# Unit 0's triangular inverse, a column solve on VectorE and a merge, replaced by five squarings on TensorE

## The chip, the cores and the metric

The kernel runs on one core of a Trainium2 chip. The metric is the device time of one execution in microseconds (us), the median of several runs. Three runs of the kernel before are given: 1079.76, 1079.80 and 1079.98 us. The engines are named PE (TensorE), DVE (VectorE), ACT (ScalarE), POOL (GpSimd) and SP (SyncE, which here only issues DMAs).

## The reference

Two stages. The first is a recurrence over 768 tokens for 4 batches and 8 heads with a 40 x 40 state each; the second is a mixture of 4 experts over the 3072 x 320 result.

```python
for t in range(S):
    y[:, :, t] = np.einsum('bhd,bhde->bhe', rt, state)
    Sa = np.einsum('bhde,bhe->bhd', state, at)
    state_decay = state * wt[:, :, None, :] - np.einsum('bhd,bhe->bhde', Sa, bt)
    state = state_decay + np.einsum('bhd,bhe->bhde', vt, kt)
...
for e in range(E):
    h = np.maximum(x @ w1[e], 0.0)
    out += p[:, e:e + 1] * (h @ w2[e])
```

All of it is in float32. In each chunk of 64 tokens the vectors Sa depend on one another through a strictly triangular 64 x 64 matrix F, so that a chunk needs (I - F)^-1, or something that acts as it, on a right-hand side. For the first chunk the state is zero, and that right-hand side is E V alone (E are the masked products of a and k, V the values).

## The kernel before

**Tiling.** A unit is one chunk of 64 tokens for two batches (tokens of both on the 128 partitions) and 8 heads: 16 matrices of 64 x 64. There are 24 units; units 0 and 1 are the first chunk. `within(q)` (line 462) makes what a unit needs inside its chunk: G, the running products of the decay w (transposes at line 286, scan at line 512), their reciprocals (529), N and K (556, 561), a scaled by G (565), their transposes on PE (535), and the products F ("pfe", 585) and E ("pe", 598). `substitute(q, eng)` (638) gathers the diagonal 32 x 32 blocks of F (643, 651, 663, 667) and solves them column by column in Z, two columns at a time, 16 rounds of a multiply (681) and a reduction (692); units 0 and 1 do it on DVE, the others on POOL. `merge(q)` (704) turns the solved blocks (709, 710), places them in QT (716) and makes the off-diagonal block with two sets of matmuls (pY, pQ). `step(q)` (742) multiplies the inverse with the right-hand side ("psat", "pst"), makes the outputs Y and the new state ("pxr", "pdy", lines 800 to 835), and brings Y into xT, the input of the mixture ("pxT", 841 to 846). `mixture_of_unit` (914) and `mixture_of_chunk` (982) are the experts' dense products ("ph", "po", "p"): they need xT and are most of PE's work.

**Products of quadrants.** `quadrants` (443) issues 32 matmuls of 64 x 64 on four quarters of the PE array, into two PSUM banks. All matmuls are issued through one helper, so their line is always 110 (transposes on PE: 113).

**Order.** Instructions of one engine that are kept in program order run in the order in which the main sequence (lines 1127 to 1214) calls the generators with `run(gen, n)`, n stages at a time; all PE instructions are, and most of DVE's in the first units (`pin`). For later DVE work a list (`VECTOR_ORDER`) states the order, and a few more pairs are stated at line 1341. What isn't kept in order is placed by the tile framework's scheduler. Before the first dense product the sequence also issues dummy matmuls (`keep_warm`, in lots of 16, 10, 20, 8 and 10), sets constants for the placing of Y on POOL (`set_pick`, 164), and loads weights on SP's queue in pieces; the third piece waits for the first Y of unit 0 (line 1343).

**PSUM and tiles.** There are five banks with the tag "big" and three with "mm". The tiles that the change uses take tags of tiles that are idle in the beginning ("hs", "a6", "F", "step", "xT", "osb").

## Time and profile before

| what | number | from |
|---|---|---|
| median of the runs | 1079.8 us | times |
| span of the profiled execution | 1077.3 us | page |
| lying around the span (median less span) | 2.5 us | worked out |
| PE busy | 1062.5 us, 99% of the span | page |
| DVE, ACT, POOL busy | 758.3, 353.2, 494.3 us | page |
| matmuls "ph" (first dense product) | from 43.82 us on | timeline |
| unit 0: first F product, first multiply of the solve, last reduction | 13.43, 19.35, 29.84 us | timeline |
| unit 0: first "psat", first Y, "pxT" | 34.19, 40.03, 40.87 us | timeline |

The page gives no device time of the profiled execution besides its span, so a change of the span is carried over to the median as it is. In a group's line the columns are: line, engine, operation, output and inputs with their shapes, the number of instructions, busy time in us, mean ns of one, and the idle time before them with what ended it. In the timeline they are start, duration, line, operation and shapes, the number of instructions merged into the row, and in brackets the idle time before them. In a table by stage each engine's busy time (and number of instructions) stands in a row for a stretch of time; PEclk is the TensorE clock granted, 1.00 being full speed.

### The profile page before, as it was taken

The page shows a single profiled execution, that of the slowest core. Times are in us where ns is not written, and L with a number is a line of the kernel's source. Part 1 is how long each engine was busy: PE and PEld are TensorE (multiplying, and loading weights), DVE is VectorE, ACT ScalarE, POOL GpSimd, SP SyncE. Part 2 cuts the span into 40 slices and gives each one's busy share as a digit, 9 for nine tenths or more (in the row PEclk, how much of TensorE's full clock was granted, in tenths as well). Part 3 has the DMA queues.
Part 4 walks back from the last instruction along what each step waited for, and adds up shares of the span by engine and source line. Part 5 has one row for each costly group of instructions (what it writes and reads, how often), then busy time and mean ns, then how long its engine had stood idle before and what let it go on. Part 6 is the DMA issues. An engine that isn't in the chain of part 4 may idle for free.

```text
span 1077.3 us, 38510 instructions
## 1 busy us (share of the span) xinstructions
PE 1062.5 (99%) x16140; PEld 955.1 (89%) x16140; DVE 758.3 (70%) x1549; ACT 353.2 (33%) x958; POOL 494.3 (46%) x1276
## 2 busy tenths in 40 slices
PE   7999999999999999999999999999999999999998
PEld 7878878899898999999999999999999999998887
DVE  7787679897676776876776768668767776634343
ACT  3433444422432423324333333233243333221110
POOL 5117777747254374363462653733735626520000
PEclk9999999999999999999999999999999999999999
DMA  7776644444444434443353263353343331121220
GB/s 129 192 202 129 142 108 108 101 85 102 103 103 104 104 92 85 115 99 79 91 129 80 59 155 62 83 128 81 90 106 86 96 89 58 54 82 42 84 76 13
DMA packets 258070, 105.81 MB, mean 98 GB/s; under 512 B 212536, under 2 KB 237672, under 8 KB 257896
## 3 DMA queue, kind: packets, MB, share of 16 engines
q1 hardware_dynamic: 253912, 102.51, 40.8%
q8 instruction: 127, 2.08, 0.8%
q10 hardware_dynamic: 3984, 0.84, 0.5%
q14 instruction: 47, 0.39, 0.1%
HBM read 95.40 MB, written 3.93 MB: 92 GB/s over the span
## 4 chain that ended last, share of the span: by engine, by line
PE 93%; DVE 3%; DMA 1%; ACT 1%; issue 1%; SPq 0%; POOL 0%; ACTq 0%; DVEq 0%
PE ph L110 40%; PE p L110 31%; PE pdy L110 3%; PE po L110 3%; PE pxr L110 2%; PE psat L110 2%; PE prn L110 2%; PE pfe L110 2%; PE pc L110 1%; PE pev L110 1%; PE pQ L110 1%; PE pe L110 1%; PE pNT L113 1%; PE pg L113 1%; PE pKT L113 1%; PE pY L110 1%
## 5 line engine op out<-in xcount | busy, mean ns | idle before, releaser
L698 POOL TENSOR_TENSOR Z<-Z 128x31 f32<-128x31 f32 (+7 forms) x704 | 263.8, 375 | 55.2
L1014 DVE TENSOR_TENSOR a<-hs 128x512 f32<-128x512 f32 x220 | 150.7, 703 | 111.6 <-ACT hs L888 111.6
L110 PE MATMUL ph<-xT,w1a 128*128 128x256 f32 (+3 forms) x1536 | 221.3, 374 | 1.7 <-issue 1.7
L888 ACT ACTIVATE hs<-ph 128x512 f32<-128x512 f32 (+1 forms) x208 | 116.9, 564 | 323.5 <-PE ph L110 323.1
L110 PE MATMUL ph<-xT,w1b 128*128 128x256 f32 (+3 forms) x1536 | 222.0, 374 | 0.0
L110 PEld LDWEIGHTS ph<-xT,w1a 128*128 128x128 f32 (+1 forms) x1536 | 167.9, 161 | 30.6 <-issue 9.5
L110 PEld LDWEIGHTS ph<-xT,w1b 128*128 128x128 f32 (+1 forms) x1536 | 168.8, 161 | 26.9 <-issue 6.1
L681 POOL TENSOR_TENSOR Z<-M,Z 128x62 f32<-128x62 f32 (+7 forms) x352 | 142.8, 406 | 98.0 <-DVE M L667 72.1
L110 PE MATMUL p<-sums,a 128*128 128x160 f32 x1056 | 164.9, 299 | 0.0
L903 DVE SCALAR_TENSOR_TENSOR osb<-p,gate,osb 128x320 f32<-128x320 f32 (+1 forms) x243 | 108.1, 481 | 79.2 <-PE p L110 72.9
L110 PEld LDWEIGHTS p<-sums,a 128*128 128x128 f32 x1056 | 152.8, 190 | 2.2
L648 POOL COPY below<-F 32x256 f32<-32x256 f32 x48 | 21.4, 445 | 227.5 <-ACT F L591 225.8
L110 PEld LDWEIGHTS p<-w,hs 128*128 128x128 f32 x704 | 98.6, 190 | 8.5 <-issue 7.3
L110 PE MATMUL p<-w,hs 128*128 128x160 f32 x704 | 104.9, 302 | 0.0
L110 PE MATMUL p<-w,a 128*128 128x160 f32 x704 | 102.8, 299 | 0.0
L110 PEld LDWEIGHTS p<-w,a 128*128 128x128 f32 x704 | 98.0, 190 | 0.0
L716 POOL COPY QT<-QTc 32x256 f32<-32x256 f32 x96 | 40.3, 420 | 71.6 <-DVE QTc L710 65.3
L808 ACT COPY RS<-pxr 64x256 f32<-64x256 f32 x88 | 32.3, 367 | 101.2 <-DVE SX L460 78.8
L629 ACT COPY EV<-pev 64x160 f32<-64x160 f32 x96 | 23.1, 286 | 90.5 <-PE pev L110 90.1
L529 DVE RECIPROCAL gp<-gp 128x320 f32<-128x320 f32 x24 | 51.6, 2152 | 0.7
L651 DVE STREAM_TRANSPOSE M<-blocks 128x1024 f32<-128x1024 f32 x24 | 47.3, 1969 | 2.9 <-ACT blocks L643 2.8
L460 DVE COPY_PREDICATED VC<-mask_up,pc 128x256 f32<-128x256 int32 x48 | 18.7, 443 | 38.4 <-PE pc L110 38.4
(153 smaller groups left out, 1389.4 us busy)
## 6 DMA issues: line engine op xcount, KB each, us to landing
w1a<-in_moe_w_dram SPq DMA_DIRECT2D x37, 512.0 KB
w1b<-in_moe_w_dram SPq DMA_DIRECT2D x37, 512.0 KB
w<-in_moe_w_dram SPq DMA_DIRECT2D x4, 1280.0 KB
w1a<-in_moe_w_dram SPq DMA_DIRECT2D x74, 64.0 KB
w1b<-in_moe_w_dram SPq DMA_DIRECT2D x74, 64.0 KB
natW<-in_w_dram SPq DMA_DIRECT2D x48, 80.0 KB
natB<-in_b_dram SPq DMA_DIRECT2D x48, 80.0 KB
natK<-in_k_dram SPq DMA_DIRECT2D x48, 80.0 KB
```

The costliest lines, as they stand in the source:

```text
L110: return stated(nc.tensor.matmul(**k))
L113: return stated(nc.tensor.transpose(**k))
L529: pin(noted(nc.vector.reciprocal(out=gp[:], in_=gp[:]), "1/gp", q.u))
L629: nc.scalar.copy(out=of_slot(q.EV[half(p)], i ^ p)[:, :, 0:D], in_=pev[i][half(p)])
L651: ins = nc.vector.transpose(out=M[:], in_=cols)
L681: ins = eng.tensor_tensor(out=Z[:, 1:3, 0:n, j + 1:Q], in0=M[:, j:j + 2, None, j + 1:Q].to_broadcast([P, 2, n, m]), in1=Z[:, here, 0:n, j: ...
L698: eng.tensor_tensor(out=z[:, 0], in0=z[:, 0], in1=z[:, x], op=ALU.add)
L716: ins = nc.gpsimd.tensor_copy(out=q.QT[quarter(i), :, quarter(i % 2)], in_=QTc[quarter(i)])
L808: nc.scalar.copy(out=RS[half(s), x ^ s::2], in_=prs[x][half(s)].rearrange("p (j i) t -> p j i t", i=2),)
L888: ins = nc.scalar.activation(out=h[:, i * HF // 2:(i + 1) * HF // 2, 0:n], in_=ph[i][:], func=ACTF.Relu,)
L903: ins = nc.vector.scalar_tensor_tensor(out=to, in0=p, scalar=sc, in1=to, op0=ALU.mult, op1=ALU.add)
L1014: ins = nc.vector.tensor_tensor(out=t[:], in0=x, in1=y, op=op)
```

## The change

For unit 0 alone the column solve, the merge and the separate products are gone. With F strictly lower triangular of size 64, (I - F)^-1 is the product of (I + F^(2^k)) for k = 0 to 5. `first_chain` makes F and its transpose U with masks on DVE, squares both five times with `quadrants` (the last time U alone), adds the unit matrix to each U on POOL (`plus_one`), and applies the factors to E V one after the other (`applied`). The factors 0 to 4 are applied there; the last one takes the place of QT in "psat" and "pst" of `step`. Copies out of PSUM are dealt to ACT (bank 0) and DVE (bank 1).

Besides that, unit 1's part of `within` is cut into more stages (its reciprocal in two halves, its transposes of V and R behind them), and the main sequence deals these stages between unit 0's. The dummy matmuls after the first two lots are gone, the constants of `set_pick` are made in two parts, and the loads of unit 2's raw w come later on SP's queue, behind the first two weight pieces. In `step`, unit 0's state update is a stage of its own behind Y. The state, unit 1's solve and everything from the first dense product on stay as they are.

```diff
+    lowf = sb.tile([P, L], FP32, name="lowf", tag="s", bufs=3)
+    nc.vector.memset(lowf[:], 1.0)
+    eye = sb.tile([P, L], FP32, name="eye", tag="xT", bufs=2)
+    nc.gpsimd.memset(eye[:], 0.0)
+    for q in range(2):
+        o = slice(q * L, (q + 1) * L)
+        nc.gpsimd.affine_select(
+            out=lowf[o], in_=lowf[o], pattern=[[-1, L]], compare_op=ALU.is_gt, fill=0.0, base=0, channel_multiplier=1,
+        )
+        nc.gpsimd.affine_select(
+            out=eye[o], in_=eye[o], pattern=[[-1, L]], compare_op=ALU.not_equal, fill=1.0, base=0, channel_multiplier=1,
+        )
...
     def set_pick():
         nc.gpsimd.memset(pick, 0.0)
...
+                    yield
...
+    tc.keep_in_program_order(nc.vector.tensor_copy(out=mask_low[:], in_=lowf[:]))
...
+    def half_at(k, s, i):
+        return i ^ (s & k & 1)
+    def at_level(t, k, j, s, i, n=64):
+        slot = half_at(k - 1, s, i) if k else s
+        return t[half(half_at(k, s, i)), slot, j, 0:n]
+    def first_chain(q, NT, KT, places, masks):
+        pairs = []
+        def pair():
+            t = sb.tile([P, HF, 2 * P], FP32, name="FU", tag="hs", bufs=3)
+            pairs.append(four_halves(t[:]))
+            return t
+        nc.gpsimd.memset(pair()[:], 0.0)
+        yield
+        def engines():
+            return enumerate((nc.scalar.copy, nc.vector.tensor_copy))
+        def out_of(to, p, n=L):
+            for r, move in engines():
+                tc.keep_in_program_order(move(out=to[:, r, :, 0:n], in_=p[r]))
+        def squared(name, k, lhs, rhs):
+            return quadrants(banks(name), 0, BY_TOKENS, L, lambda j, s, i: (
+                half_at(k, s, i), half_at(k + 1, s, i), j, at_level(lhs, k, j, s, i), at_level(rhs, k, j, s, i),
+            ))
+        def plus_one(k):
+            t = sb.tile([P, 2 * NJ, L], FP32, name="UI", tag=("a6", "F")[k % 2])
+            ins = nc.gpsimd.tensor_tensor(
+                out=t[:], in0=pairs[k][:, 1].rearrange("p r j e -> p (r j) e"),
+                in1=eye[:, None, :].to_broadcast([P, 2 * NJ, L]), op=ALU.add,
+            )
+            tc.keep_in_program_order(ins)
+            return in_slots(t[:])
+        def applied(k, x, to):
+            p = quadrants([of_mixture(f"px{r}") for r in range(2)], 0, BY_TOKENS, D, lambda j, s, i: (
+                half_at(k, s, i), half_at(k + 1, s, i), j, at_level(one_plus[k], k, j, s, i),
+                at_level(x, k, j, s, i, D),
+            ))
+            out_of(to, p, D)
+            return to
+        tc.keep_in_program_order(nc.scalar.copy(out=q.VC[:, :, 0:D], in_=n_tokens(q)))
+        pf = quadrants(banks("pfe"), 0, BY_TOKENS, L, lambda j, s, i: (
+            s, i, j, of_slots(q.AT, s, j, i), of_pairs(NT, s, j, i),
+        ))
+        pu = quadrants(banks("pu"), 0, BY_TOKENS, L, lambda j, s, i: (
+            s, i, j, of_pairs(NT, s, j, i), of_slots(q.AT, s, j, i),
+        ))
+        pe = quadrants([of_mixture(f"pe{r}") for r in range(2)], 0, BY_TOKENS, L, lambda j, s, i: (
+            s, i, j, of_pairs(KT, s, j, i), of_slots(q.AT, s, j, i),
+        ))
+        for to, data, mask in ((pairs[0][:, 0], pf, mask_low), (pairs[0][:, 1], pu, mask_up)):
+            for r in range(2):
+                ins = nc.vector.copy_predicated(
+                    out=to[:, r], mask=mask[:, None, :].to_broadcast([P, NJ, L]), data=data[r],
+                )
+                tc.keep_in_program_order(ins)
+        one_plus = [plus_one(0)]
+        ET = ETs()
+        for s in range(2):
+            tc.keep_in_program_order(causal(of_slot(ET[:], s), pe[s]))
+        VT = sb.tile([P, 2 * NJ, L], FP32, name="VT", tag="turned", bufs=3)
+        q.RT = sb.tile([P, 2 * NJ, L], FP32, name="RT", tag="RT", bufs=2)
+        moves = []
+        for x, t, p in (("V", VT, big("pVT")), ("R", q.RT, of_mixture("pRT"))):
+            turn(f"p{x}T", tok(q.n["padded" + x]), False, p)
+            for at, (o, p_) in enumerate(places(t, p)):
+                moves.append(lambda o=o, p_=p_, x=x, at=at: tc.keep_in_program_order(
+                    noted(nc.scalar.copy(out=o, in_=p_), x + "Tc", q.u, at)))
+        for move in moves[:3]:
+            move()
+        yield
+        X = None
+        for k in range(4):
+            F, U = pairs[k][:, 0], pairs[k][:, 1]
+            p = squared("pfe", k, U, F), squared("pu", k, F, U)
+            pair()
+            for x in range(2):
+                out_of(pairs[k + 1][:, x], p[x])
+            one_plus.append(plus_one(k + 1))
+            if k < 3:
+                moves[3 + k]()
+            if k == 0:
+                q.EV = EVs()
+                pev = [of_mixture(f"pev{r}") for r in range(2)]
+                for j, s, i in BY_TOKENS:
+                    at = (s * NJ + j) * D
+                    matmul(
+                        out=pev[i][half(i), at:at + D], lhsT=ET[half(i), head(j, s), :],
+                        rhs=q.VC[half(i), head(j, s), 0:D], start=True, stop=True,
+                    )
+                X = in_slots(q.EV[:])
+                for i, move in engines():
+                    ins = move(
+                        out=X[half(i), :, :, 0:D],
+                        in_=pev[i][half(i), 0:H * D].rearrange("p (r j e) -> p r j e", r=2, j=NJ),
+                    )
+                    tc.keep_in_program_order(ins)
+            else:
+                to = sb.tile([P, 2, NJ, 64], FP32, name="X", tag="step", bufs=3)
+                X = applied(k - 1, X, to[:])
+            yield
+        F, U = pairs[4][:, 0], pairs[4][:, 1]
+        pu = squared("pu", 4, F, U)
+        pair()
+        out_of(pairs[5][:, 1], pu)
+        q.one_plus = plus_one(5)
+        to = sb.tile([P, 2, NJ, 64], FP32, name="X", tag="step", bufs=3)
+        X = applied(3, X, to[:])
+        yield
+        pc = quadrants(banks("pc"), 0, BY_TOKENS, L, lambda j, s, i: (
+            d_half(j, s), i, j, of_slots(VT, d_half(j, s), j, i, D), of_slots(q.RT, d_half(j, s), j, i, D),
+        ))
+        q.X = applied(4, X, in_slots(RHs()[:]))
+        yield
+        masks(pc)
+        yield
...
         if q.u == 1:
-            yield
-            VT = turn_rv("V")
-            yield
-            turn_rv("R")
             yield
...
         pg = turn("pg", tok(Gv), q.u == 2, of_mixture("pg") if q.u == 1 else None)
+        if q.u == 1:
+            yield
         pg = by(pg[:], 64)[:, :, 0:D]
         gp = sb.tile([P, H, D], FP32, name="gp")
         pin(noted(nc.vector.tensor_tensor(out=gp[:], in0=pg, in1=n["W"][:], op=ALU.mult), "gp", q.u))
-        pin(noted(nc.vector.reciprocal(out=gp[:], in_=gp[:]), "1/gp", q.u))
-
-        yield
+        for hs in (slice(0, NJ), slice(NJ, H)) if q.u == 1 else (slice(0, H),):
+            pin(noted(nc.vector.reciprocal(out=gp[:, hs], in_=gp[:, hs]), "1/gp", q.u))
+            yield
+        if q.u == 1:
+            VT = turn_rv("V")
+            yield
+            turn_rv("R")
+            yield
...
+        if q.u == 0:
+            yield from first_chain(q, NT, KT, places_of, masks)
+            return
...
-            RH = q.EV
+            RH = q.EV if q.u else None
...
+        def rhs_at(j, s, i, n=64):
+            return RH[half(i ^ s), head(j, s), 0:n] if q.u else at_level(q.X, 5, j, s, i, n)
+        def inverse_at(j, s, i):
+            return q.QT[half(i ^ s), head(j, s), :] if q.u else at_level(q.one_plus, 5, j, s, i)
         psa = quadrants(p, 0, BY_TOKENS, L, lambda j, s, i: (
-            i ^ s, d_half(j, s), j, RH[half(i ^ s), head(j, s), :], q.QT[half(i ^ s), head(j, s), :],
+            i ^ s, d_half(j, s), j, rhs_at(j, s, i), inverse_at(j, s, i),
         ))
         SX = SXs()
         if not q.end:
-            at = (banks("pst"), 0) if q.start else (p, NJ * L)
+            at = (p, NJ * L)
+            if q.start:
+                at = (banks("pst") if q.u else [of_mixture(f"pst{x}") for x in range(2)], 0)
             pst = quadrants(*at, BY_TOKENS, D, lambda j, s, i: (
-                i ^ s, i, j, q.QT[half(i ^ s), head(j, s), :], RH[half(i ^ s), head(j, s), 0:D],
+                i ^ s, i, j, inverse_at(j, s, i), rhs_at(j, s, i, D),
             ))
...
             noted(nc.vector.tensor_tensor(out=Y[:], in0=Y[:], in1=Gv, op=ALU.mult), "YG", q.u)
+        if q.u == 0:
+            yield
         if not q.end:
...
     norm = normalize()
+    pick_set = set_pick()
     keep_warm(16)
     run(ws[0], 1)
     go(load_raw(units[1], "W"))
     run(ws[0], 1)
     keep_warm(10)
     run(ws[0], 1)
-    run(ws[1], 1)
     for x in "VR":
         load_padded(units[1], x)
     load(units[1], "WBK")
     go(load_raw(units[1], "A"))
-    go(load_raw(units[2], "W"))
     load_probs()
     load_piece()
     load_piece()
     load_w2(order_of(-1)[0])
+    run(ws[0], 1)
+    run(pick_set, 9)
+    run(ws[0], 1)
+    def scores_of(u):
+        run(ws[u], 1)
+        yield
+    run(ws[0], 1)
+    run(ws[1], 1)
+    go(load_raw(units[2], "W"))
     load_piece()
     load_piece()
     run(ws[0], 2)
-    keep_warm(20)
-
-    def scores_of(u):
-        run(ws[u], 1)
-        yield
-
-    substitute(units[0], nc.vector, scores_of(0))
+    run(ws[1], 1)
     run(ws[0], 1)
-    set_pick()
-    m, s = merge(units[0]), begin_step(0)
-    run(m, 1)
+    run(ws[1], 1)
     run(ws[0], 1)
-    keep_warm(8)
-    run(norm, 1)
-    run(ws[1], 1)
-    keep_warm(10)
     load(units[2], "W")
     for x in "VR":
         load_padded(units[2], x)
-    run(m, 1)
+    run(ws[1], 1)
+    run(ws[0], 1)
+    run(pick_set)
+    run(ws[1], 1)
+    run(ws[0])
+    s = begin_step(0)
+    run(s, 2)
+    go(load_raw(units[2], "A"))
+    run(norm, 1)
+    run(s, 1)
     run(ws[1], 2)
-    run(ws[0])
-    run(ws[1], 2)
-    run(m)
-    go(load_raw(units[2], "A"))
-    run(s, 3)
     run(ws[1], 1)
     run(s, 1)
     run(ws[1], 1)
+    run(s, 1)
     run(s)
+    run(ws[1], 1)
     load(units[2], "BK")
     load_w2(order_of(-1)[1])
     load_piece()
...
-    for one, then in [*zip(names, names[1:]), *((f"out{n}", x) for n, x in moved), ("blocks0.3", "VCv1"), ("blocks0.3", "ETc0.0"), ("blocks1.3", "Zu1.0"), ("blocks1.3", "Zu1.3"), *turned_ahead, *in_second, *waits_of_scalar]:
+    for one, then in [*zip(names, names[1:]), *((f"out{n}", x) for n, x in moved), ("SXc0.3", "VCv1"), ("SXc0.3", "VTc1.0"), ("blocks1.3", "Zu1.0"), ("blocks1.3", "Zu1.3"), *turned_ahead, *in_second, *waits_of_scalar]:
```

## The prediction

> **What bounds the kernel now.** The page first: PE is the bound, but a busy PE is not the whole answer, because dummy matmuls count as busy.

> ```profile
> PE 1062.5 (99%) x16140; PEld 955.1 (89%) x16140; DVE 758.3 (70%) x1549; ACT 353.2 (33%) x958; POOL 494.3 (46%) x1276
> ```

> So I cut the span where the first dense product "ph" starts, 43.82 us, in the table by stage (columns: stretch, then PE, PEld, DVE, ACT, POOL busy, clock, DMA).

> ```profile
> 0.00:43.82 43.82, 36.68 (x600) 33.48 (x604) 34.50 (x84) 17.45 (x48) 20.50 (x60) 0.96 0.75 153
> 43.82:200.00 156.18, 154.78 (x2670) 129.49 (x2660) 122.09 (x249) 61.48 (x180) 91.98 (x229) 1.00 0.59 139
> 600.00:800.00 200.00, 200.00 (x3172) 182.71 (x3171) 149.28 (x304) 68.80 (x188) 95.26 (x249) 1.00 0.43 99
> ```

> Behind 43.82 us PE is idle for 1.4 us in the next 156 and not at all later; its order is fixed and its work there isn't changed. So the time is "when the first ph starts, plus a constant", and the question is when it starts. The chain of waits (start, duration, what) tells what leads up to it:

> ```profile
> 13.43 0.77 PE pfe L110 x32
> ...
> 17.90 0.70 DVE Z L663
> ...
> 29.92 0.11 DVE Z L692
> ...
> 30.71 0.45 DVE QTc L710
> ...
> 32.96 0.41 POOL QT L716
> ...
> 37.15 0.46 DVE SX L460
> ...
> 44.00 5.30 PE ph L110 x64
> ```

> The reader is to see that from 14 to 31 us the chain is DVE's solve of unit 0, then the merge, then the step. Every microsecond taken out of this stretch lets ph start earlier, as long as unit 1's pc and pfe, which stand ahead of ph in PE's order (42.38 to 43.8), come earlier too.

> **What goes.** From F's arrival in PSUM (14.17) to the mask SX (37.15) the chain takes 22.98 us: blocks, M and its products to 19.3; 16 rounds to 30.03; Qc, QTc and the merge to 34.2; psat and pxr to 37.15. The first three go. ACT's copies and POOL's select of ET go as well (1.3 us on POOL, off the path), and 38 of the dummy matmuls, which filled idle time.

> **What comes, step by step**, with these rows (mean ns behind the bar):

> ```profile
> L501 DVE COPY RT<-pRT 128x256 f32<-128x256 f32 x1 | 0.4, 424 | 3.3 <-PE pRT L113 3.3
> L460 DVE COPY_PREDICATED VC<-mask_up,pc 128x256 f32<-128x256 int32 x10 | 3.9, 441 | 4.1 <-PE pc L110 4.1
> L565 POOL TENSOR_TENSOR AT<-AT,G 128x512 f32<-128x512 f32 x1 | 1.3, 1280 | 0.0
> ```

> A set of 32 quarter matmuls follows the next after 0.46 us (pfe 42.89, pe 43.36), and its result is in PSUM 0.74 us after its start (13.43 to 14.17).
> 1. Masked copies of F and U: four on DVE, two take 0.78: 1.6 us. First squaring at 15.8. ACT's VT copies, PE's transposes of V and R and DVE's ET lie beside.
> 2. One level: F's product, U's product behind it (ready after 1.20), DVE's copy of U 0.42, 0.05 to PE: 1.7 us. Level 0 has the pev matmuls behind it on two quarters only; not shown before, between 0.46 (four quarters) and 0.92. I take 0.9: level 0 is 1.8 us, to 17.6.
> 3. Level 1: DVE runs EV's copy (0.45), then unit 1's moved G transposes (0.93), gl and G0 (0.27), from 17.8 to 19.45, before it copies F and U (0.84): to 20.3. The move costs 1.0 us; before, these sat in a gap at 13.29.
> 4. Level 2: to 22.0.
> 5. Level 3: DVE copies X (0.3), then unit 1's scan (1.24; before, it sat behind QTc). The scan reads two SBUF operands, and POOL's addition "I + U" of this level starts at the same moment. What happens then is in the timeline:

> ```profile
> 37.29 1.28 POOL L565 TENSOR_TENSOR AT<-AT,G 128x512 f32<-128x512 f32 x1
> 37.83 1.09 DVE L556 SCALAR_TENSOR_TENSOR n_tok<-natB,gp 128x320 f32<-128x320 f32 x1
> ```

> The same n_tok took 0.49 us at 11.49, with only the 0.37 us selects on POOL; here it ends 0.35 after POOL's. So the scan is taken to wait for POOL, 0.95 us (bounds: nothing, and 1.28): scan to 24.5, copies to 25.35. POOL's addition with a broadcast operand isn't in the trace; I take 1.28, the row of the same shape, between the memset of that shape (0.53) and 1.4 (512/320 of k_tok's 0.87).
> 6. Level 4, U alone: X (0.3), unit 1's AT transpose (0.70), U's copy 0.42 to 26.8, the last addition 1.28 to 28.05. Beside it pg, pc and the last `applied` on PE.
> 7. psat from 28.1: 0.74, SaT 0.65, pxr 0.74: 30.35. DVE meanwhile: gp 0.45, half the reciprocal 1.08, VC's masks 0.78: 30.4. SX mask at 30.4, against 37.15: 6.75 us earlier.
> 8. SX to Y (2.88) and to pxT (0.84) as before: pxT at 34.1. The second half of the reciprocal (1.08) lies in the 2.3 us of pdy; the transposes of unit 1's V and R lie between pxr and pdy, where PE waits for SX. Unit 1's N follows Y on DVE, K and its scaling of a run on POOL from 31.5 to 33.7.
> 9. Behind pxT (1.5): pNT, pKT (0.46 each), pc; NT's copy (0.59) comes behind xT's (0.48) on ACT, to 36.95; pfe, KT's copy, pe: ph at 38.1. Before, pNT and pKT came ahead of pxT, so pxT to ph took 2.95 us and now 4.0: 1.05 us are given back.

> Sum: 43.82 - 38.1 = **5.7 us earlier**. Span 1077.3 - 5.7 = 1071.6. The median of the runs lies 2.5 us above the span, and I carry that over: 1079.8 - 5.7 = 1074.1.

> **Edits costed at nothing.** PE's 480 added quarter matmuls lie in time in which PE waits or ran dummies; without that cover each 32 cost 0.46. POOL's new constants (a memset and four selects of 0.24) and the memset of FU (twice 0.53) end near 11.6, ahead of F; the nine pick steps behind (0.74 + 8 x 0.37) end near 15.3, ahead of the first addition at 15.8; if the scheduler puts the memset behind them, 1.1 us are lost. The other selects need to be done by pxT only. SP: unit 2's four raw w loads (0.49 each) go behind the probabilities and two pieces, which are issued some 2 us sooner; unit 1's raw a is issued by 19.9 as before and needed at 25.65. The stage between Y and the state update lets N pass in front of it; the state is first read by unit 2.

> **The clock.** One stretch speaks against the change:

> ```profile
> 9.52:12.93 3.41, 2.20 (x21) 2.02 (x19) 3.38 (x4) 1.62 (x5) 3.05 (x8) 1.00 1.03 122
> ...
> 19.75:23.16 3.41, 1.49 (x26) 1.07 (x17) 3.07 (x11) 3.13 (x10) 0.00 (x0) 1.00 0.70 126
> 23.16:26.57 3.41, 3.32 (x35) 3.20 (x36) 3.10 (x10) 0.04 (x1) 0.00 (x0) 0.50 0.55 154
> ...
> 36.80:40.21 3.41, 2.77 (x78) 2.26 (x72) 1.94 (x4) 1.80 (x6) 1.77 (x2) 1.00 0.48 81
> ```

> After 3.41 us with PE busy for 44%, the next 3.41 us ran at half clock; after 64% and 81% they did not. In my schedule levels 3 and 4 are the thin place: PE is busy 22.0 to 23.55 and from 25.35 on, so a stretch of 3.41 us has between 46% and 80%, by where it begins. A drop costs what PE has on the path in the next 3.41 us, about 1.5 us (two to three of psat, pxr, `applied`, at 0.46 to 0.74 each). [...]

> **Rivals.**
> - *One or two half-clock stretches* (1.5 us each): 1075.6 to 1077.1. For it: 46% beside 44%. Against: only some positions of the stretch give that, and the other levels are 65 to 90%.
> - *The waits at levels 1 and 3 don't come* (scan ahead of POOL's addition, pev at 0.46, the scheduler uses gaps): 1 to 2 us better: 1072.1 to 1073.1. Against: DVE's order is pinned.
> - *The gain is hidden by the weights*: ph starts early and waits for w1 or w2; at worst 1079.8. Against: the DMA share falls from 1.11 (35 to 36 us) to 0.40, so the first two pieces and w2 have landed by 36; issued 2 us sooner they have by 34, ahead of 38.1. The third piece waits for unit 0's Y, which moves 6.75 us, more than ph.
> - *The change does not do what it says*: DVE stays the chain's engine, since each level needs its copies. If all of unit 1's moved DVE work (4.8 us) came on the path instead of the 3.3 counted, 1075.6; in my range.
> - *Slower*: the half clock stays. PE's work on the path from 15.8 us on is 5 x 1.2 for the squarings, 2.2 (applied, psat, pxr), 2.3 (pdy), 1.5 (pxT), 2.3 (pNT to pe): 14.3 us, which would double: 1074.1 + 14.3 = 1088.4. It decides from 40% of that work on, four stretches in a row. Against: at half clock PE is busier, and the row above is back at 1.00 after one stretch.

> **Chances.** Forecast (1073.2 to 1075): 0.52. Half-clock stretches or all of DVE's moved work on the path: 0.26. Better than 1073.2: 0.10. Gain hidden: 0.06. Slower: 0.06. What a measurement here can tell from no change is about 0.2% (2.2 us), so up to 1077.6 counts as faster: 0.52 + 0.26 + 0.10 = 0.88, less 0.01 for a third stretch: 0.87; within 0.2%: 0.07; slower: 0.06. The range takes in both ends of the unknown costs: down to 1071.8 (scan's wait gone, pev at 0.46, the additions at half their price: together 2.3 us), up to 1077.3 (two stretches).

> **What would show it.** First squaring near 15.8 and the sixth product near 25.4; levels 1 and 3 longer than 0 and 2, with DVE's G and scan as what they wait for; the scan longer than 1.24 us beside a POOL addition; SX at 30.4, pxT at 34.1, ph at 38.1; PE still not idle behind it. Wrong would be: a clock below 1.00 between 26 and 34 us, levels of more than 3 us throughout, ph waiting for a DMA, or new idle time of PE behind ph.

## The result, and the profile after

The changed kernel takes 1089.45 us (median of four runs, 1086.8 to 1090.68), the kernel before 1079.89 us on the same chip: a ratio of 1.0072, 95% interval 1.0051 to 1.0093. It is slower by 0.7%, where 1074.1 us (1071.8 to 1077.3) was predicted. Its profiled execution took 1088.4 us with a span of 1086.7, against a span of 1077.3 before.

The page of the changed kernel, its line of engines and its line of the queue that brings instructions (packets, MB, share of 16 engines):

```profile
PE 1064.7 (98%) x16512; PEld 957.2 (88%) x16512; DVE 752.3 (69%) x1532; ACT 352.0 (32%) x953; POOL 497.9 (46%) x1280
...
q8 instruction: 130, 2.13, 0.8%
```

Of the first line nothing can be read: PE still seems busy all the time. The second is the one that the prediction passed over. 2.13 MB in 130 packets are 16 KB each. The same line before the change:

```profile
q8 instruction: 127, 2.08, 0.8%
```

The table by stage, cut at the same places as before:

```profile
0.00:43.82 43.82, 31.47 (x825) 29.00 (x827) 25.31 (x58) 14.08 (x38) 23.35 (x63) 0.84 0.63 131
43.82:200.00 156.18, 152.21 (x2756) 127.31 (x2748) 118.30 (x246) 62.45 (x183) 89.90 (x224) 1.00 0.60 141
600.00:800.00 200.00, 200.00 (x3169) 182.49 (x3168) 146.00 (x299) 67.23 (x183) 101.51 (x266) 1.00 0.41 94
```

In the first 43.82 us PE, DVE and ACT do less than before: PE 31.47 us in place of 36.68, DVE 25.31 in place of 34.50. The work did leave DVE, and yet ph starts later. The clock fell from 0.96 to 0.84. The chain of waits says what is there instead:

```profile
16.02 0.62 PE pfe L110 x32
16.64 0.34 PE pu L110 x21
16.98 0.92 issue
17.90 0.37 PE pu L110 x9
...
20.43 2.02 issue
22.45 0.42 PE px L110 x10
...
25.96 2.24 DVE G L666
...
30.02 1.80 issue
31.82 0.43 PE px L110 x11
...
35.20 1.14 PE psat L110 x32
...
36.71 1.90 issue
38.61 0.86 PE pst L110 x19
...
45.69 1.61 PE pxT L110 x12
...
49.72 5.41 PE ph L110 x64
```

"issue" is time in which the engine waits for nothing that the profile shows. In the sets' names pfe and pu are the products for F and U, px those of `applied`, pev is E V. Four times PE stops in the middle of a set of 32 matmuls whose operands are all there: 0.92 + 2.02 + 1.80 + 1.90 = 6.64 us. The places are regular. From 17.90 to 22.45 PE executes the last 11 of pu, 32 pev, 32 pfe, 32 pu and 20 of the 32 px: 127 matmuls, and with each its weight load, 254 instructions. Two more in the trace are semaphore instructions, which aren't counted as busy: 256. The stretches from there to 26.19, 31.82 and 38.61 have 127 matmuls and 256 instructions each as well, and one packet of q8 comes in each. It looks as if PE had used up a block of code and waited for the next; run 1 below puts that to the test. ph starts at 49.72 in place of 44.00 (both from the chain), 5.7 us later, where 5.7 us earlier was predicted.

The clock, in slices of one microsecond:

```profile
21.00:22.00 1.00, 0.00 (x0) 0.00 (x0) 0.79 (x3) 0.00 (x0) 0.00 (x0) 1.00 0.39 77
...
23.00:24.00 1.00, 1.00 (x48) 1.00 (x46) 0.36 (x2) 0.30 (x2) 0.76 (x1) 0.50 0.18 46
...
37.00:38.00 1.00, 0.00 (x0) 0.00 (x0) 0.26 (x1) 0.07 (x1) 0.00 (x0) 0.50 0.08 9
```

Half clock holds from about 22.6 to 26.0 and from 32.9 to 43.1 us. Ahead of the first stretch stands the stop of 2.02 us (slice 21); ahead of the second a wait of 1.29 us for DVE's copies (to 29.11) and the stop of 1.80. The stop at 36.71 (slice 37) lies inside the second.

Of the 9.4 us that the span grew, 5.7 are there when ph starts. The rest comes behind it, by the waits of both traces: near 90 us ph waits 1.0 us for a weight piece, near 121 us pxr 0.7 with no releaser, in the middle of a set; at 320 to 360 us PE's clock is 0.96 (1.00 before), which by half of its 3.4 us at half clock is an estimated 1.7.

### The profile page after: what moved, and what is told of

Same layout as the page of the kernel before. It is cut to its first block, busy times and chain, and to the rows that moved or that the text cites. A ratio compares the mean times of both kernels' runs of the same rounds, so it can differ in the third digit from the quotient of the medians.

```text
span 1086.7 us, 39253 instructions
## 1 busy us (share of the span) xinstructions
PE 1064.7 (98%) x16512; PEld 957.2 (88%) x16512; DVE 752.3 (69%) x1532; ACT 352.0 (32%) x953; POOL 497.9 (46%) x1280
## 3 DMA queue, kind: packets, MB, share of 16 engines
q8 instruction: 130, 2.13, 0.8%
## 4 chain that ended last, share of the span: by engine, by line
PE 95%; issue 1%; DVE 1%; ACT 1%; DMA 1%; SPq 0%; ACTq 0%; DVEq 0%
PE ph L110 40%; PE p L110 31%; PE pdy L110 3%; PE po L110 3%; PE pxr L110 2%; PE psat L110 2%; PE prn L110 2%; PE pfe L110 2%; PE pc L110 1%; PE pev L110 1%; PE pQ L110 1%; PE pe L110 1%; PE pg L113 1%; PE pNT L113 1%; PE pKT L113 1%
## 5 line engine op out<-in xcount | busy, mean ns | idle before, releaser
L110 PE MATMUL ph<-xT,w1a 128*128 128x256 f32 (+3 forms) x1536 | 222.2, 375 | 1.8 <-issue 1.8
L110 PE MATMUL ph<-xT,w1b 128*128 128x256 f32 (+3 forms) x1536 | 222.2, 374 | 0.0
L110 PEld LDWEIGHTS ph<-xT,w1a 128*128 128x128 f32 (+1 forms) x1536 | 168.6, 162 | 30.5 <-issue 10.7
L110 PEld LDWEIGHTS ph<-xT,w1b 128*128 128x128 f32 (+1 forms) x1536 | 169.1, 162 | 26.9 <-issue 5.9
L110 PE MATMUL p<-sums,a 128*128 128x160 f32 x1056 | 165.0, 300 | 0.0
L110 PEld LDWEIGHTS p<-sums,a 128*128 128x128 f32 x1056 | 152.8, 190 | 2.2
L110 PEld LDWEIGHTS p<-w,hs 128*128 128x128 f32 x704 | 98.6, 190 | 8.5 <-issue 7.3
L110 PE MATMUL p<-w,hs 128*128 128x160 f32 x704 | 104.9, 302 | 0.0
L110 PE MATMUL p<-w,a 128*128 128x160 f32 x704 | 102.8, 299 | 0.0
L110 PEld LDWEIGHTS p<-w,a 128*128 128x128 f32 x704 | 98.0, 190 | 0.0
L860 POOL COPY QT<-QTc 32x256 f32<-32x256 f32 x92 | 37.9, 412 | 58.7 <-DVE QTc L854 55.1
L686 DVE RECIPROCAL gp<-gp 128x320 f32<-128x320 f32 (+1 forms) x25 | 51.8, 2071 | 0.7
L476 DVE COPY_PREDICATED VC<-mask_up,pc 128x256 f32<-128x256 int32 x48 | 18.6, 442 | 40.1 <-PE pc L110 38.1
```

Of the source, the lines that this page charges most:

```text
L110: return stated(nc.tensor.matmul(**k))
L686: pin(noted(nc.vector.reciprocal(out=gp[:, hs], in_=gp[:, hs]), "1/gp", q.u))
L860: ins = nc.gpsimd.tensor_copy(out=q.QT[quarter(i), :, quarter(i % 2)], in_=QTc[quarter(i)])
```

## The experiments

TensorE's code is counted in instructions of the trace. An fp32 product of a quarter leaves four there, two matmuls and the weight load of each, so a set of 32 is 16 products and 64 instructions. "ph at" is the start of the first ph in the timeline (before 43.82, after 49.54). It and the stops are read from one profiled execution of each kernel; in runs 2, 5, 12 and 14 that was the longest of the kernel's executions (1092.36, 1094.43, 1090.04 and 1090.30 us), so there it stands for more than the median. A ratio is to the kernel before on the same chip, whose median lay between 1080.3 and 1081.8 us. A piece is half of one expert's w1, and w2 is an expert's second matrix.

**1. The added matmuls without their data.** The kernel before, with independent quarter matmuls of a constant in place of its 20 dummies, 8 sets of 32, and the same again late:

```
-    keep_warm(20)
+    quads(banks("quad"), 8)
...
+        if u == 8:
+            quads(banks("quad"), 8)
```

> The kernel before, with the 20 dummy matmuls of 128x128 at 14.5 us replaced by 8 sets of 32 independent quarter matmuls (256 matmul records with as many loads of weights, 3.7 us at 0.46 us a set), and 8 more such sets put among the dense products at about a third of the span. None of them waits for data, and none is read. Theory of the code blocks (in the profile of the changed kernel PE stops four times in the middle of a set, 128 records and 128 loads apart, 0.9 to 2.0 us each, and one 16 KB packet of the instruction queue lies ahead of each stop): both places show one or two stops of about 1 to 3 us with no releaser ('issue'), 128 records apart. Rival (the stops are waits for copies, or the draining of the array between shapes): the sets run without a stop, 3.7 to 4 us each lot. If the stops come only beside heavy DMA, the early lot has them and the late one, where the DMA share is about 0.4, doesn't.

Measured: 1092.69 us, one run. The timeline, early and late:

```profile
17.97 2.10 PE L110 MATMUL quad<-ident 64*64 64x64 f32 x128 [1.47 <-issue]
...
22.25 0.74 PE L110 MATMUL quad<-ident 64*64 64x64 f32 x34 [2.18 <-issue]
...
347.97 2.10 PE L110 MATMUL quad<-ident 64*64 64x64 f32 x128 [0.55 <-issue]
...
351.70 1.04 PE L110 MATMUL quad<-ident 64*64 64x64 f32 x56 [1.63 <-issue]
```

The matmuls wait for nothing and nothing waits for them, and PE still stops after each 128. 128 matmuls and their 128 weight loads are 256 instructions, and the packets of the instruction queue are 16 KB each. They last 2.10 us, and the next block starts 4.28 us (early, with a DMA share of 0.61 in between) or 3.73 us (late, with 0.26) after the one before. So a stop here is no wait for data: these quarter matmuls use up code faster than it comes. ph is at 46.54, 2.7 us later than before; where the rest of the 12.4 us of this one run comes from isn't followed here.

**2. Is it the clock?** Four dummies of 128x128, written into the bank that is used next, ahead of the squarings 2 to 5, psat, pxr and pxT:

```
-            return quadrants(banks(name), 0, BY_TOKENS, L, lambda j, s, i: (
+            p = banks(name)
+            held(p[0], hold)
+            return quadrants(p, 0, BY_TOKENS, L, lambda j, s, i: (
```

> The changed kernel, with 4 dummy matmuls of 128x128 (0.12 us each at full clock, 16 machine instructions) ahead of each squaring from the second on, of psat, pxr and pxT, written to the bank that the following set overwrites. Theory of the clock (PE below 46% busy in some stretch of 3.4 us halves the clock, and that is most of the loss): clock 1.00 through the chain, ph some 5 us earlier than 49.5, time near 1084. Theory of the code blocks (stops first, clock second): the stops stay, 1 to 2 us each, the clock may still drop, ph at 47 to 49, time 1086 to 1089.

Measured: 1089.35 us, ratio 1.0084 (1.0058 to 1.011); ph at 52.01. Both theories had ph earlier than that. The first stretch at half clock is gone, the second is not (34.7 to 44.9 us). It follows a longer stop than any in the changed kernel; the 28 dummies are 112 instructions of code themselves:

```profile
33.23 0.40 PE L110 MATMUL pu<-FU 64*64 64x64 f32 x12 [2.93 <-issue]
```

The clock as a cause by itself is not shown, and not excluded by this run.

**3. SP's order.** In the changed kernel SP stands 13.1 us, to 45.66, behind the third piece, which waits for unit 0's Y, and unit 2's loads stand behind it. Here they go ahead of the piece, as before the change:

```
+    load(units[2], "W")
+    for x in "VR":
+        load_padded(units[2], x)
     load_piece()
     load_piece()
```

> The changed kernel, with unit 2's loads of W, V and R put in the program ahead of the third weight piece. In the changed kernel SP's queue stood still from 32.9 to 45.66 us behind that piece, which waits for unit 0's Y, and these loads came behind it; later, at 90.4 us, ph waited 1.0 us for a piece. Theory that this order costs time behind the first ph: that wait goes, time 1 to 2 us lower; ph's start the same, or up to 1 us later, since the loads then lie beside the fetch of code. Rival (the late wait comes from ph's late start alone): no difference.

Measured: 1089.97 us, ratio 1.0098 (1.0077 to 1.0118), ph at 50.24. The 1.0 us wait at 90 us is gone, others came (ph for ACT's blocks 1.6, pdy for code 0.9), and the time is as before this edit. SP's order alone is not it.

**4. The weights later.** First piece behind the third squaring's copies:

```
-    for k, then in ((2, "Y0.0"), (served[22], "SX5.0")):
+    for k, then in ((0, "third0"), (2, "Y0.0"), (served[22], "SX5.0")):
```

> The changed kernel, with the first weight piece, and so everything behind it on SP's queue, waiting for the copies of the third squaring (about 25 us instead of 23.2). If the fetch of a code block is slowed by the weights' transfers on the same DMA engines (a block took 3.7 to 4.6 us from its predecessor's first instruction while the DMA share was 0.4 to 0.8, and 5.6 and 6.8 us while it was 0.9 to 1.1), the blocks up to the third squaring come as before or sooner and the later ones are slowed as much; ph changes by less than 1 us either way, and the stop in the middle of the last squaring's px shortens only if the weights start after its block was asked for. If the fetch doesn't depend on the transfers: the same four stops at the same places.

Measured: 1087.34 us, ratio 1.0064 (1.0049 to 1.0079); ph at 47.95, 1.6 us earlier, where less than 1 us was expected, with the first piece issued at 24.32 in place of 23.18. The stops are 1.04, 1.76, 1.48, 1.73 and 1.44, but the block that came at 31.82 comes at 30.50, and the first stretch at half clock is gone. Part of it is given back, po waits 1.9 us for w2.

**5. More code.** One more set of 32 quarter matmuls ahead of the squarings 2 to 5, 256 instructions:

```
+            if extra:
+                quads(p)
```

> The changed kernel, with one set of 32 independent quarter matmuls (64 machine instructions, 0.46 us of PE) ahead of each of the squarings 2 to 5, written to the banks that the squaring overwrites. The run with 4 dummies of 128x128 there (16 machine instructions, 0.47 us) had ph at 52.0 us in its profile. Theory of the code blocks: 256 machine instructions more are one block more, one stop more, and ph 4 us or more behind the changed kernel's 49.5, near 54; time near 1094. Theory that PE's or DVE's time sets the chain: PE's 0.46 us lies in the waits for the copies, as the dummies' did; ph and time within 2 us of the changed kernel.

Measured: 1091.09 us, ratio 1.0089 (1.0061 to 1.0116). One block more, a fifth stop (0.65, 1.70, 1.96, 2.51, 3.54), and ph at 54.38, 4.8 us later, as expected. The profiled execution took 1094.43 us, near the 1094 expected, but the median rose by less (1091.1).

**6. Less code.** The powers from the second on in bf16, whose product is one matmul and one load (sets of 16 in the trace), 224 instructions fewer in all:

```
-            t = sb.tile([P, HF, 2 * P], FP32, name="FU", tag="hs", bufs=3)
+            t = sb.tile([P, HF, 2 * P], BF16 if pairs else FP32, name="FU", tag="hs", bufs=3)
```

> The changed kernel, with the powers of F from the second on kept in bfloat16 for the squarings (the powers that are added to I and applied are rounded to bfloat16 too, which changes the result slightly). The trace shows an fp32 matmul of the program as two records and two loads; in bfloat16 it is expected as one of each, so the seven sets of the squarings 2 to 5 are 224 machine instructions less, 0.9 of a block. Theory of the code blocks: ph 3 to 4 us earlier, 45 to 46 us, time 1083 to 1086. Theory of the clock: PE does less, so the clock drops as before or more; ph 1 us earlier at most.

Measured: 1085.51 us, ratio 1.0035 (1.0021 to 1.0048), ph at 45.97, as expected. Stops 0.70, 0.29 and 1.32, but 17 us at half clock (23.0 to 40.1).

**7. Three squarings.**

```
-        for k in range(4):
+        for k in range(2):
...
-        F, U = pairs[4][:, 0], pairs[4][:, 1]
+        F, U = pairs[2][:, 0], pairs[2][:, 1]
```

> The changed kernel with three squarings instead of five: the factors of the 16th and 32nd power of F are left out of the product. That takes away six sets (squarings and applied), 384 machine instructions, 1.5 blocks, and by the prediction's own levels 3.35 + 2.7 us less what is left of unit 1's DVE work (2 us), 4 us. Theory of the code blocks: 1.5 blocks of 4.3 us, ph 6 us earlier, near 43.5, time near 1082. Prediction's theory alone: 4 us earlier, near 45.5.

Measured: 1083.85 us, ratio 1.0023 (1.0006 to 1.004), ph at 43.28, as expected. Stops of 0.77, 2.02, 1.09 and 1.18; 10.2 us at half clock (28.6 to 38.9). Even with two of five squarings gone, ph starts only where it did before the change.

**8. Both.** Three squarings and bf16 powers:

> Both: three squarings (the 16th and 32nd power's factors are left out) and bfloat16 powers from the second on (rounded). Three sets are 96 machine instructions less than with three squarings in fp32. Theory of the code blocks: another 1.5 us, ph near 42, ahead of the kernel before (43.8); time 1078 to 1081. Theory of the clock: no earlier than with three squarings.

Measured: 1082.01 us, ratio 1.0003 (0.9991 to 1.0015), no difference from before; ph at 43.08 where 42 was expected, and a time above the 1078 to 1081 expected. So 480 instructions fewer bring ph 6.5 us forward, but 13.7 us still lie at half clock (24.8 to 35.1, 38.5 to 41.9).

**9 and 10. The clock again, with less code.** Dummies in the places where run 6 and run 8 waited; for run 10, ahead of the third squaring, psat and pxT:

```
-        pu = squared("pu", 2, F, U)
+        pu = squared("pu", 2, F, U, 10)
...
+            held(p[0], 5)
...
+                held(px, 6)
```

> The changed kernel with the bf16 powers of the run with less code, and 128x128 dummies in the places where that run's TensorE waited: 10 ahead of the third squaring, 10 ahead of the fifth, 4 ahead of psat, 6 ahead of pxT. 30 dummies are some 120 machine instructions, under half a block. Without them: TensorE at half clock from 23.0 to 40.0 us, ph at 45.97, 1085.51 us. Theory 'blocks first, then the clock': with fewer instructions the half clock now has a price of its own, since TensorE's work between 23 and 40 us is one chain; the dummies keep the clock above 0.9 over 20 to 40 us, ph starts at 42 to 43.5, and the time is 1081 to 1083. Rival 'the stops alone': the clock is kept but ph stays within 1 us of 45.97 and the time within 1 us of 1085.5. Rival 'dummies do not keep the clock': the clock is half for over 8 us between 23 and 40 as without them.

> The run with three squarings and bf16 powers (it leaves out the factors with the 16th and the 32nd power), with dummies: 10 ahead of the third squaring, 5 ahead of psat, 6 ahead of pxT, some 84 machine instructions. Without them: half clock from 25 to 35.2 and 38.8 to 41.5 us, ph at 43.08, 1082.01 us, the same as the kernel before. Theory 'blocks first, then the clock': the clock stays above 0.9 over 20 to 40 us, ph starts at 38.5 to 40.5, and the time is 1078 to 1080, at or below the kernel before. Rival 'the stops alone': ph within 1 us of 43.1 though the clock is kept. Rival 'given back behind ph': ph earlier by 2.5 us or more, but the time within 1 us of 1082, with waits for weights behind ph in its place.

Measured: run 9 1086.81 us, ratio 1.0054 (1.0042 to 1.0066), ph at 45.88 (45.97 without the dummies); run 10 1082.33 us, ratio 1.0023 (1.0005 to 1.0042), ph at 43.44 (43.08). In run 9 the clock is 1.00 in every slice from 14 us to past ph. Its timeline has, at pdy:

```profile
38.86 0.46 PE L111 MATMUL pdy<-VC,k_tok 64*64 64x104 f32 x5 [3.10 <-issue]
```

and run 10's chain:

```profile
25.91 1.00 PE psat L111 x9
26.91 1.13 issue
28.04 0.69 PE psat L111 x32
...
31.42 0.59 PE pdy L111 x17
32.00 3.31 issue
35.32 1.69 PE pdy L111 x44
```

psat is back at 0.69 us (1.14 at half clock in the changed kernel). PE does these matmuls in little over half the time and then stands longer: 3.10 us at most in run 9, 1.32 in run 6. For run 9 "the stops alone" holds by ph and the clock; its time is 1.3 us off, on another chip. In run 10 ph fits that rival too, but the clock was kept only up to the stop of 3.31 us; then it dropped, here in a slice behind it:

```profile
36.00:38.00 2.00, 2.00 (x34) 1.75 (x26) 1.00 (x3) 0.00 (x0) 0.00 (x0) 0.57 0.03 8
```

The dummies are 120 and 84 instructions of code themselves, so these two runs can't say what the full clock would be worth if it cost no code.

**11 and 12. The blocks without the weights.** Runs 10 and 9, with the first piece behind ACT's copies of SaT:

```
-            nc.scalar.copy(out=SaT[:, :, x, :], in_=psa[x])
+            noted(nc.scalar.copy(out=SaT[:, :, x, :], in_=psa[x]), "SaTc", q.u, x)
...
-    for k, then in ((2, "Y0.0"), (served[22], "SX5.0")):
+    for k, then in ((0, "SaTc0.1"), (2, "Y0.0"), (served[22], "SX5.0")):
```

> The run with three squarings, bf16 powers and dummies (it leaves out the factors with the 16th and the 32nd power), with one more edit: the first weight piece is issued behind ACT's copies of SaT (about 29 us) in place of 22.5 us. Without it: the block of code that TensorE needs at pdy came while the DMA engines were busy for 97% and more with the weights (28 to 33 us), TensorE stood 3.31 us, ph at 43.44, 1082.33 us. Theory 'the blocks pace TensorE, and weights in flight slow the blocks': the stop at psat (1.13) and that at pdy (3.31) fall to under 0.5 and under 1.0 us, ph starts at 40 to 41.5, and the time is 1079 to 1081.5, the same as the kernel before, with up to 1 us of new waits for w2 or the third piece. Rival 'a block takes as long without the weights': the stop at pdy stays over 2.5 us and ph within 0.7 us of 43.4. Rival 'given back': ph at 41.5 or earlier, and a time within 1 us of 1082.3, with over 2 us of new waits for weights behind ph.

> The run with bf16 powers and dummies and all five squarings, with the same edit: the first weight piece behind ACT's copies of SaT (about 33 us). Without it: stops of 0.77, 0.33, 0.20 and 3.10 us, clock 1.00 throughout, ph at 45.88, 1086.81 us. Theory 'the blocks pace TensorE, and weights in flight slow the blocks': the stop at pdy falls to under 1.5 us, since only the last block is then requested beside the weights, ph starts at 43 to 44.5, and the time is 1084 to 1086. Rival 'a block takes as long without the weights': a stop of over 2.5 us stays and ph stays within 0.7 us of 45.9. Rival 'given back': ph at 44.5 or earlier, time within 1 us of 1086.8 or above, with over 2 us of new waits for weights behind ph.

Run 11's first ph and its second po, in the timeline:

```profile
37.20 2.60 PE L111 MATMUL ph<-xT,w1a 64*64 64x128 f32 x32
...
59.27 7.11 PE L111 MATMUL po<-w,hs 128*128 128x320 f32 x16 [6.14 <-DMA w<-in_moe_w_dram]
```

The stops at psat and pdy are gone altogether, and ph starts at 37.20, 6.2 us earlier than in run 10 and 6.6 earlier than before the change. The table by stage shows what was taken away (last columns: clock, DMA share, GB/s). Run 10, then run 11:

```profile
28.00:30.00 2.00, 1.96 (x88) 1.88 (x91) 0.19 (x1) 1.19 (x5) 0.00 (x0) 1.00 0.97 245
30.00:32.00 2.00, 2.00 (x53) 1.65 (x45) 1.52 (x3) 1.94 (x7) 0.00 (x0) 1.00 1.00 341
32.00:34.00 2.00, 0.00 (x1) 0.00 (x0) 0.29 (x1) 1.30 (x4) 1.63 (x2) 1.00 1.14 300
```

```profile
26.00:28.00 2.00, 1.97 (x73) 1.76 (x71) 1.97 (x4) 0.31 (x3) 0.00 (x0) 1.00 0.01 2
28.00:30.00 2.00, 2.00 (x51) 1.87 (x44) 0.81 (x3) 1.93 (x9) 0.00 (x0) 1.00 0.18 33
30.00:32.00 2.00, 2.00 (x68) 1.70 (x66) 1.21 (x2) 1.92 (x7) 0.71 (x1) 1.00 0.84 291
```

With the DMA engines nearly free while PE works up to psat (shares of 0.01 and 0.18 from 26 to 30 us, in run 10 0.75 and 0.97), PE stops nowhere there. And yet the run takes 1085.06 us, ratio 1.0035 (1.0021 to 1.005). From the first ph to the end its profiled execution takes 1046.3 us, the kernel before 1033.5. Of these 12.8 us po's wait for w2 is 6.1. In the wait and behind it the clock is half, from 57.6 to 64.5 us, and po takes 7.11 us (4.58 in the kernel before, at full clock):

```profile
60.00:64.00 4.00, 4.00 (x9) 2.63 (x8) 0.00 (x0) 0.00 (x0) 0.00 (x0) 0.50 1.07 313
```

Run 12, with five squarings, has no stop between 26 us and ph, and ph at 42.27 in place of 45.88; its profiled execution waits 2.2 us for w2 and 4.4 for a piece. It takes 1085.51 us, ratio 1.0045 (1.0028 to 1.0063). So the theory was right on the stops in both. Run 11's time misses its range and even what "given back" allowed (by 1.8 us); run 12's lies inside the theory's range, but with ph earlier than the theory had it and with the waits that "given back" names.

**13 and 14. Is that only the order of the loads?** Runs 11 and 12, with the second expert's w2 ahead of unit 2's loads:

```
+    load_w2(order_of(-1)[1])
     load(units[2], "W")
...
-    load_w2(order_of(-1)[1])
```

> The run with three squarings whose first piece is issued behind SaT (it leaves out the factors with the 16th and the 32nd power), with one more edit: the second expert's w2 is loaded ahead of unit 2's W, V and R (about 39 us) in place of behind all of unit 2's loads (52.09 us). Without it: ph at 37.20, but the second po waited 6.14 us for that w2, and 1085.06 us. Theory 'two walls, code blocks in front of ph and the weights behind it, and the second is only an order on the queue': the wait of 6.1 us is gone, ph stays at 37 to 38, and the time is 1078 to 1080.5, as the kernel before or up to 2 us below it. Rival 'the bytes bind': the second po still waits for over 2 us, or a wait for the third or fourth piece of over 2 us comes in its place, and the time stays at 1082 or above.

> The run with all five squarings, bf16 powers, dummies and the first piece behind SaT, with the same edit: the second expert's w2 ahead of unit 2's W, V and R (about 43 us) in place of 53.79 us. Without it: ph at 42.27, waits of 2.16 us for w2 and 4.36 us for the piece behind it, 1085.51 us. Theory 'only an order on the queue': both waits fall to under 1 us in sum, ph stays at 42 to 43, and the time is 1080 to 1083. Rival 'the bytes bind': the waits for weights behind ph stay over 3 us in sum and the time at 1084 or above.

Run 13 took 1085.44 us, ratio 1.0034 (1.0022 to 1.0046), run 14 1087.82, ratio 1.0056 (1.0039 to 1.0073). The waits for w2 fell to 0.5 us and to nothing, and others came, ph's among them; run 13's timeline:

```profile
60.52 1.42 PE L111 MATMUL ph<-xT,sums 64*64 64x128 f32 x16 [2.49 <-DMA sums<-in_moe_w_dram]
...
85.59 2.83 PE L111 MATMUL ph<-xT,sums 64*64 64x128 f32 x32 [2.37 <-DMA sums<-in_moe_w_dram]
```

and run 14's:

```profile
88.69 5.23 PE L111 MATMUL ph<-xT,sums 64*64 64x128 f32 x32 [5.55 <-DVE VT L302]
```

Run 13 is the rival "the bytes bind": the piece used at 60 us is issued at 55.67 where it was issued at 50.56 before the change. Its first w1 piece went out at 28.26 (before 23.65), and from there to 57 us SP issues one load behind the other but for one pause (39.47 to 42.68). Run 14 is neither: PE waits for no weights, but ph stands behind DVE's work on unit 3, and that had waited 3.17 us, to 84.22, for unit 3's raw w; those loads were issued from 78.99, in run 12 from 77.23. That this second wall can't be moved by any order is not shown; the orders tried did not.

## Why the prediction was wrong, step by step

**The step that failed** is the first sentence of "Edits costed at nothing": "PE's 480 added quarter matmuls lie in time in which PE waits or ran dummies; without that cover each 32 cost 0.46." Time of PE was there; code was not. The price of 0.46 us for 32 (14.4 ns for one) held here only inside a block. A block of 128 fp32 quarter matmuls lasts 2.10 us at full clock (run 1), and where a stop shows when the next one came, it came 3.73 and 4.28 us after the one before in run 1, and 4.55, 5.63 and 6.79 in the changed kernel (from 17.90 to 22.45, 26.19 to 31.82, 31.82 to 38.61). So 32 of them cost an estimated 0.9 to 1.7 us where they piled up, by a quarter of these times. In the trace of before this could not be read from the rows that the prediction took: two sets in a row (pfe, pe) fit into a block. The runs stand in that order: ph at 54.4 us with 256 instructions more, 52.0 with 112 more, 49.5, 46.0 with 224 fewer, 43.3 with 384 fewer, 43.1 with 480 fewer.

**A second step failed** behind it: "when the first ph starts, plus a constant". In run 11 ph starts 6.6 us earlier than before the change, and the profiled execution is 6.2 us longer (1083.5 for 1077.3). So an earlier ph doesn't carry over to the end by itself. Run 11 leaves out two factors and loads the weights 4.7 us later than the kernel before, so how much of its 5.7 us the prediction's own schedule would have kept stays open. Nor is PE "not at all" idle behind 200 us in the kernel before: it is busy for 397.41 of the 400 us to 600.

Steps 1 to 9, predicted against the chain and timeline of after:
- *First squaring 15.8*: 16.0. Right.
- *Level 0 to 17.6*: 18.9. The 32 pev took about 1.0 (0.9 taken); a stop of 0.92 is most of the rest.
- *Level 1 to 20.3, longest by DVE's moved work*: 22.6, with a stop of 2.02 and not DVE as what ends it. DVE's copies behind its moved work end at 21.81 here, so about 1.4 of the 2.02 us lie beside a wait that would have been there anyway.
- *Level 3: the scan waits 0.95 us for POOL's addition of 1.28*: right as a time. The scan took 2.31 us beside the addition, 1.07 over its 1.24. That it stood still for the addition is the author's estimate; the rows show the overlap and the two times:

```profile
25.83 1.28 POOL L518 TENSOR_TENSOR UI<-FU,eye 128x512 f32<-128x512 f32 x1 [1.32 <-PE px L110]
25.88 2.31 DVE L666 TENSOR_TENSOR_SCAN G<-G,first 128x512 f32<-128x512 f32 x1
```

- *psat 28.1, SX 30.4, pxT 34.1*: 35.2, 41.2, 45.69. pxT is 11.6 us late. By an estimate about 5.2 are the stops (6.64 less the 1.4 at level 1), about 4 the half clock from 32.9 to 43.1 (10.2 us less the stop of 1.90, of which half would do at full clock), and about 1 that from 22.6 to 26.0 (level 2 took 2.6 us in place of 1.7).
- *pxT to ph 4.0*: 4.03 (45.69 to 49.72). Right; PE's clock is 1.00 again.
- *Behind ph nothing*: wrong by 3.7 us. "SP: ..." had unit 2's loads and w2 out of the sum; SP stood 13.1 us behind the piece that waits for Y. Run 3 shows that this order alone is not what the time hangs on. The first piece was issued 0.5 us sooner than before (23.18 for 23.65), not some 2.

**The clock.** The paragraph saw the thin place and the price of a drop, but took the stretches of idleness from waits for data (at most 1.8 us) and bounded them by one or two drops. The sum of 1074.1 has the full clock throughout, which no row shows for that schedule; measured ahead of ph were two drops, of 3.4 and 10.2 us. The stops made most of the idle time. None of after's stops is over 2.02 us, and the clock was halved. The stretch of before behind which it was halved, PE busy for 44%, has no longer gap either:

```profile
22.48 0.34 PE L110 MATMUL pc<-RT,VT 40*64 40x64 f32 x8 [1.58 <-ACT RT L503]
```

In the changed kernel PE was busy for 1.39 us (41%) and 1.62 us (47%) of the 3.41 us ahead of its two drops, and for 2.04 to 3.17 us in the stretches of that length between 8.98 and 29.46 that ran at full clock with no drop behind them. Behind the stop of 3.10 us in run 9 the clock stayed at 1.00, behind that of 3.31 in run 10 it dropped.

**The rivals.** The slower one (1088.4, the half clock stays) has nearly the measured number, in part by luck: half clock is there, and by the estimate above it is some 5 of the 11.6 us at pxT, not 14.3, with the stops as the rest. The first drop came behind a stop, which that rival didn't have. Run 9, with the clock at 1.00 and 120 instructions of dummies for it, has ph where run 6 has it at half clock. How much the half clock would cost if code came in time isn't settled. "Gain hidden by the weights" was given 6% for the first ph, where no DMA was waited for; runs 11 to 13 show it as the second wall, at po and the next pieces, once the first is taken away. It was looked for in the wrong place: not whether the first pieces land, but whether w2 and the pieces behind them still come in time.

## What to carry to other kernels

Before you put work on TensorE as many small fp32 matmuls, count its instructions and not only its time: in these traces four for an fp32 product and two for a bf16 one, and where PE stopped, a block of 256 took 3.73 us at best (run 1) and 6.79 beside weights (the changed kernel). Look for "issue" in the middle of a set, and for the instruction queue's packets, before the clock; a clock that was restored by more instructions brought nothing back here (ph at 45.88 in run 9, 45.97 in run 6). When a stage is brought forward, follow the transfers two uses behind it, since issuing the weights 5.8 us later gave ph 6.2 us in run 11 and cost po a wait of 6.1 and the half clock behind it.
